# Half of the second MoE's output product in seven products, W_out of the first unit taken chunk by chunk, and a table that moves every group of a planned order

## The chip, the cores and the metric

The kernel runs on one core of one Trainium2 chip. The metric is the device time of one execution in microseconds (us); lower is better. The engines are TensorE (PE in the profile; its weight loads are PEld), VectorE (DVE), ScalarE (ACT), GpSimd (POOL) and SyncE (SP), which issues the DMAs.

## The reference

Three steps run one after the other; all inputs are fp32 or fp64 arrays.

```
q, k, v: (4, 8, 576, 64)            tau: scalar
scores = q @ k.T / 8;  keep scores >= max - tau;  attn = softmax of what is kept;  x = attn @ v
x  -> (2304, 512)
MoE 1:  r = relu(x @ w_in);   y = (s * r * r + b) @ w_out          # w_in (512, 2048), w_out (2048, 512)
MoE 2:  h = y @ w_in2;        out = (h * sigmoid(1.702 * h)) @ w_out2
```

## The kernel before

**Stages.** There are four batches of 576 tokens. Attention runs in eight units of 256 tokens (two for each batch, four head pairs each); the 64 last tokens of each batch are collected into a ninth unit. Unit 0 goes through MoE 1 in fp32 (`pair32`, then `bank32`), units 1 to 8 in pairs of fp16 parts, three matmuls for each product (`pair` L977, then `bank` L1065). MoE 2 runs over four blocks of 512 tokens and one of 256.

**MoE 2.** Its hidden product for a 512-token block is already done in seven products for each two by two group of quarters (`hidden7`, L1277, 256 columns a matmul, 8 calls of 42 matmuls a block); the 256-token block uses `hidden2` (L1333, 192 matmuls of 256 columns). The activation (`tanh`, L1229 on ScalarE and L1234 on VectorE) is cut into a high and a low fp16 part (L341 on ScalarE, L1240 on VectorE), which are the tiles `g`. The output product `rows2` (L1364) makes 128 tokens at a time: 48 matmuls of 512 columns, over four chunks of W_out with 12 each, 18 times in all. ScalarE scales the result (L341), and SyncE stores it.

**Weights.** Weights arrive as fp64 words of 8 bytes in `wst` tiles, are rebuilt as fp32 (`convert`, L778) and cut into fp16 parts. For W_out of MoE 1 this waits until unit 0, which uses the fp32 form, is done: `mlp` puts the four norms and one `scale_out` behind unit 0, and that cuts all four chunks in a row (`split_w`: 16 times L341 on ScalarE and L863 on VectorE).

**The order.** `Plan` holds every step with its engines, estimated cost and priority, and plays them forward: each engine takes the ready step of the lowest priority number whose buffers are free. What comes out is one fixed order for each engine, which the chip then follows with semaphores. So the estimates move no time by themselves; they move instructions. Priorities come from due times in the table `KN`. PSUM has four single banks `a`, one `d`, and three rotating ones (`y`, `yy`, from `bank_of`) in the last stage.

## Time and profile before

| | |
|---|---|
| median of 3 runs | 1019.95 us (1019.66 to 1020.05) |
| profiled execution, its own time | 1023.23 us |
| its span, first to last instruction | 1021.5 us |
| PE busy | 979.0 us (96%) |
| DVE busy | 694.9 us (68%) |
| ACT busy | 622.8 us (61%) |
| POOL busy | 207.3 us (20%) |
| granted TensorE clock, mean | 0.992 |

The span leaves 1.73 us of the profiled execution's own time outside. A matmul's recorded duration is a pipelined one: what a row of matmuls costs TensorE is read from the chain of work, where a run of them has its length and its count, not from the mean of one.

### The profile page before, as it was taken

To read this page: it belongs to the slowest core of one execution; us is meant where nothing else is said; L and a number is where in the kernel's file an instruction comes from. 1 tells how busy PE (TensorE), PEld (TensorE's weight loads), DVE (VectorE), ACT (ScalarE), POOL (GpSimd) and SP (SyncE) were. 2 spreads that over 40 slices of the span, in tenths; PEclk is the share of its full clock that TensorE was granted. 3 is DMA by queue.
4 is the path that set the end of the run, shared out by engine and by line. 5 is a ranking of instruction groups with operands and counts; after the bars stand their busy time and mean duration, and the time that the engine had idled before them with its cause. 6 is when DMAs were issued, how large, how long until landed. Compare 5 with 4: busy or idle time off the path is not lost.

```text
span 1021.5 us, 21133 instructions
## 1 busy us (share of the span) xinstructions
PE 979.0 (96%) x8181; PEld 723.0 (71%) x8181; DVE 694.9 (68%) x1538; ACT 622.8 (61%) x1194; POOL 207.3 (20%) x319
## 2 busy tenths in 40 slices
PE   5888999979999999999999999999999999999998
PEld 3556667757877777777778888886486486486483
DVE  5888688796778777886675888796366356356240
ACT  5777776587677666676555888694364355354250
POOL 2110034433443454444442000000001001000000
PEclk9999999999999999999999999999999999999999
DMA  7786267736668786776764257310010010000000
GB/s 258 260 287 220 68 167 176 172 66 160 123 136 210 157 165 126 151 169 144 148 105 83 93 175 237 131 49 1 32 53 1 31 53 1 31 32 1 31 12 21
DMA packets 173060, 115.84 MB, mean 113 GB/s; under 512 B 136536, under 2 KB 149920, under 8 KB 172960
## 3 DMA queue, kind: packets, MB, share of 16 engines
q1 hardware_dynamic: 172960, 114.50, 43.8%
q8 instruction: 64, 1.05, 0.4%
q14 instruction: 36, 0.29, 0.1%
HBM read 72.62 MB, written 10.00 MB: 81 GB/s over the span
## 4 chain that ended last, share of the span: by engine, by line
PE 74%; DVE 10%; ACT 7%; DMA 5%; issue 2%; POOL 0%; SPq 0%; ACTq 0%; DVEq 0%; POOLq 0%
PE a L1364 18%; PE yy L1065 11%; PE a L1277 8%; PE yy L977 7%; PE S L491 6%; PE y L977 4%; PE T L636 3%; PE y L1036 3%; PE yy L1277 3%; PE d L1277 2%; DVE e L541 2%; DMA wst<-in_moe_w_out 2%; DMA PT<-p 2%; DVE nm L515 2%; PE y L1277 2%
## 5 line engine op out<-in xcount | busy, mean ns | idle before, releaser
L977 PEld LDWEIGHTS <-wb 128*128 128x128 f16 x1536 | 147.8, 98 | 32.8 <-issue 15.9
L565 POOL TENSOR_TENSOR p<-e,p 128x512 f16<-128x512 f32 x108 | 128.5, 1190 | 204.3 <-ACT p L339 176.6
L1065 PEld LDWEIGHTS <-wb 128*128 128x128 f16 x1536 | 148.5, 98 | 26.7 <-issue 9.3
L1065 PE MATMUL yy<-g,wb 128*128 128x256 f16 x1248 | 146.3, 274 | 2.1 <-DVE g L354 1.7
L541 DVE SCALAR_TENSOR_TENSOR e<-S,tb,e 128x576 f32<-128x576 f32 x144 | 115.0, 814 | 47.4 <-ACT e L537 44.0
L1364 PE MATMUL a<-wb,g 128*128 128x512 f16 x648 | 145.2, 379 | 0.0
L1277 PEld LDWEIGHTS <-l 128*128 128x128 f16 x1344 | 131.5, 98 | 19.2
L515 DVE TENSOR_REDUCE nm<-S 128x1 f32<-128x576 f32 x144 | 104.5, 749 | 29.9 <-PE S L491 29.7
L1364 PEld LDWEIGHTS <-g 128*128 128x128 f16 x648 | 63.4, 98 | 72.1
L537 ACT ACTIVATE e<-S,tb 128x576 f32<-128x576 f32 x108 | 76.4, 735 | 56.7 <-DVE tb L529 47.1
L977 PE MATMUL yy<-xs,wb 128*128 128x256 f16 x888 | 104.2, 273 | 0.0
L1277 PE MATMUL a<-xs,l 128*128 128x256 f16 x768 | 96.4, 273 | 0.0
L339 ACT ACTIVATE p<-e 128x576 f16<-128x576 f32 x108 | 73.0, 677 | 32.9 <-DMA PT<-p 22.8
L977 PE MATMUL y<-xs,wb 128*128 128x256 f16 x648 | 78.6, 273 | 7.3 <-ACT gt L984 7.3
L341 ACT ACTIVATE gt<-a,x2y 128x512 f32<-128x512 f32 x18 | 12.4, 688 | 88.0 <-PE a L1364 64.8
L354 POOL TENSOR_TENSOR st<-wb 128x512 f32<-128x512 f32 x5 | 7.1, 1418 | 276.3 <-DVE gt L1234 123.0
L491 PE MATMUL S<-kk,qa 64*128 64x288 f32 (+1 forms) x320 | 54.6, 445 | 8.2 <-ACT kk L388 8.2
L1229 ACT ACTIVATE gt<-wb,x2h 128x256 f32<-128x256 f32 x64 | 36.4, 609 | 40.4 <-DVE wb L1296 37.8
L491 PE MATMUL S<-kk,qb 64*128 64x288 f32 (+1 forms) x320 | 57.6, 453 | 1.5 <-DVE e L541 1.4
L1289 ACT ACTIVATE wb<-a 128x256 f32<-128x256 f32 x96 | 36.3, 379 | 30.2 <-PE a L1277 29.7
L778 DVE SCALAR_TENSOR_TENSOR wb<-wst,tw 128x512 int32<-128x512 int32 x64 | 45.5, 713 | 6.6 <-ACT tw L339 6.0
L1364 PE MATMUL a<-wb 128*128 128x512 f16 x216 | 49.4, 379 | 0.0
(184 smaller groups left out, 1589.2 us busy)
## 6 DMA issues: line engine op xcount, KB each, us to landing
wst<-in_moe_w_in SPq DMA_DIRECT2D x32, 512.0 KB
wst<-in_moe_w_out SPq DMA_DIRECT2D x32, 512.0 KB
rv<-in_v SPq DMA_DIRECT2D x32, 320.0 KB
kk<-in_k SPq DMA_DIRECT2D x32, 288.0 KB
qb<-in_q SPq DMA_DIRECT2D x16, 288.0 KB
yd<-gt SPq DMA_DIRECT2D x18, 256.0 KB
wb<-yd SPq DMA_DIRECT2D x16, 256.0 KB
out<-gt SPq DMA_DIRECT2D x16, 256.0 KB
```

Of the source, the lines that this page charges most:

```text
L339: nc.scalar.activation(dst(), src(), AF.Copy)
L491: nc.tensor.matmul(Sp[to, half, :HALF], q[h][r, qcols], k[r, h * HALF : (h + 1) * HALF])
L515: {"DVE": 668.0}, lambda _: nc.vector.tensor_reduce(nm.ap, Sv(), AX.XY, ALU.min), [Sp], [nm],
L537: lambda _: nc.scalar.activation(ev(), Sv(), AF.Exp, bias=nm.ap if plain else nb(), scale=-1.0), [Sp, biased], [e],
L541: lambda _: nc.vector.scalar_tensor_tensor(ev(), Sv(), tb(), ev(), ALU.is_le, ALU.mult, accum_out=p["acc"][:, i, 0:1]),
L565: nc.gpsimd.tensor_tensor(p16[:, S + H2 :], e[:, :MAIN], p16[:, :MAIN], ALU.subtract)
L778: lambda _: nc.vector.scalar_tensor_tensor(stage[:, j, :].bitcast(I32), st.ap.bitcast(I32)[:, 1:1025:2], 13, flat(), ALU.logical_shift_rig ...
L977: nc.tensor.matmul(hps[:, h, :], W[:, i, j, kk * P : (kk + 1) * P], x[:, k, kk, :], start=t == 0, stop=t == len(terms) - 1,)
L1065: nc.tensor.matmul(yp[:, h, :], self.W[0, 1, c][:, i, j, i0 * P : (i0 + 1) * P], u["g"][c][:, k, j, :], start=t == 0, stop=t == len(terms) ...
L1229: lambda _, cols=cols, h=h: nc.scalar.activation(gt[:, cols], h(), AF.Tanh, scale=th[:, c : c + 1]),
L1277: nc.tensor.matmul(to(bank), W[:, u, m, j, kk * P : (kk + 1) * P], y[:, v, z, kk, :], start=n == 0 and not more, stop=n == 5, skip_group_c ...
L1364: nc.tensor.matmul(yp(), part(f, k), self.W[1, 1, f // CH][:, w, f % CH, :], start=n == 0, stop=n == 47,)
```

## The change

Five things differ. (1) Of MoE 2's W_out, chunks 2 and 3 (`pairs7`) are held as seven combinations (`seven_out`), the activations that meet them too (`seven_g`, four sums or differences and seven cuts for two rows of tiles), and `rows7` makes two tiles of 128 tokens together: 48 matmuls of 512 columns for chunks 0 and 1, and seven products of 12 matmuls of 256 columns for chunks 2 and 3. (2) The 256-token block goes through `hidden7` too, with 128 columns a matmul. (3) Unit 0 takes W_out of MoE 1 chunk by chunk for both output banks (`rows32`), the norms and scales stand ahead of it, and each chunk is cut behind its last use (`part_out`). (4) s and b are loaded behind the first k and q, and a one-column Exp on ScalarE stands at the start. (5) A table `MOVES` shifts the priority of each of some 760 groups of steps, several cost estimates are raised, and there are more buffers (`g` 8 for 6, `gt` 4 for 3, two of the `g` tiles lent from `wst`).

```diff
-    1, "g": 6, "wb": 9, "xs": 4, "gt": 3, "son": 1, "xon": 1, "gw": 1, "hs": 0.58, "hk": 2.1, "h4": 4, "scan": 2,
+    1, "g": 8, "gl": 2, "r7": 2, "no": -3.0, "rk": 0.5, "gon": 1, "wb": 9, "xs": 4, "gt": 4, "son": 1, "xon": 1, "gw": 1, "hs": 0.58, "hk": 2.1, "h4": 4, "scan": 2,
...
+MOVES = [
+    7, -135, -223, 203, 520, -20, 23, 47, 139, 20, -365, -464, -313, -1172, -1249, -1063, -1044, -412, -80, -123,
...
+        op["prio"] += 100.0 * MOVES[self.group] if self.group < len(MOVES) else 0.0
...
-        for i, src in enumerate((self.tau, self.s, self.b)):
-            nc.sync.dma_start(sc[:, i : i + 1], src.partition_broadcast(P))
-        self.s_ap, self.b_ap = sc[:, 1:2], sc[:, 2:3]
+        nc.sync.dma_start(sc[:, 0:1], self.tau.partition_broadcast(P))
+        warm = pool.tile([P, 1], F32, name="warm")
+        nc.scalar.activation(warm, self.ones[:, 0:1], AF.Exp)
...
+        if p["unit"] == p["hp"] == 0:
+            for i, src in ((1, self.s), (2, self.b)):
+                self.load(lambda i=i: self.scal_t[:, i : i + 1], lambda src=src: src.partition_broadcast(P), [self.scal], P * 4)
...
-        W = Buf(self.lp, "l16", [P, 2, 8, 2, 256], F16, NCH)
+        W = Buf(self.lp, "l16", [P, 2, 7, 2, 256], F16, NCH)
...
-        for c, stage in enumerate(stages):
-            self.W[m, 1, c] = self.split_w(stage, lambda c=c: sv["o"][:, c : c + 1], [sv["o"]])
+    def part_out(self, m, c, stage):
+        sv = self.scale_of(m)
+        scale = lambda: sv["o"][:, c : c + 1]
+        if m and c in self.pairs7:
+            self.W[m, 1, c] = self.seven_out(stage, scale, sv["o"])
+        else:
+            self.W[m, 1, c] = self.split_w(stage, scale, [sv["o"]])
+    def seven_out(self, stage, scale, scaled):
+
+        tiles = [Buf(stage.pool, stage.tag, [P, 2, 4, 2, 256], F16, stage.bufs) for _ in range(2)]
+        place = {name: (tiles[i // 4], i % 4) for i, name in enumerate(self.RIGHT)}
...
+        self.seven_b(
+            lambda name, src, reads: self.parted(*place[name], src, scale, reads + [scaled], place[name][1]),
+            b11, b12, b21, b22, t2, t3, q, of, 512,
+        )
+        return place
...
-    def bank32(self, u, ib):
+    def rows32(self, u, c):
...
+        if c == 0:
+            u["y"] = [self.bank_of([P, 2, n]) for _ in range(2)]
+        W, g = self.stage[0, 1, c], u["g"][c]
+        for ib, yp in enumerate(u["y"]):
+            for h in range(2):
...
+        if c in self.pairs7:
+            if r:
+                self.seven_g(blk, c, j, blk.pop("first"), gt)
+            else:
+                blk["first"] = gt
+            return
...
+    def seven_g(self, blk, c, j, g0, g1):
+
+        half = blk["n"] // 2
+        place = self.g7_of(blk, c, j)
+        of = lambda g, k: (lambda: g[:, k * half : (k + 1) * half])
+        a11, a21, a12, a22 = of(g0, 0), of(g0, 1), of(g1, 0), of(g1, 1)
+        p11, p21, p12, p22 = (g0, 0), (g0, 1), (g1, 0), (g1, 1)
+        cut = lambda name, src, part: self.parted(*place[name], src, 2.0 ** -18, [part], place[name][1], half)
+        any = dict(on=("DVE", None, "POOL")[KN["gon"]])
+        cut("a22", a22, p22)
+        self.sub(a22, a21, a22, [p21], [p22], half, op=ALU.add, **any)
+        cut("s1", a22, p22)
+        self.sub(a21, a11, a21, [p11], [p21], half, **any)
+        cut("a11", a11, p11)
+        self.sub(a11, a22, a11, [p22], [p11], half, **any)
+        cut("s3", a21, p21)
+        cut("a12", a12, p12)
+        self.sub(a12, a12, a11, [p11], [p12], half, **any)
+        cut("s2", a11, p11)
+        cut("s4", a12, p12)
+
...
-    def hidden2(self, blk, f):
...
+    def rows7(self, blk, t, pace):
...
+        Y, a, b = [self.single("a"), self.single("a")], self.single("d"), self.bank_of([P, 512])
+        flat = [c for c in range(NCH) if c not in self.pairs7]
...
+                    {"PE": (pe16(12, 512), 60.0)}, mm, [self.W[1, 1, c], tiles[c, 0][0], tiles[c, 1][0]] + [Y[r]] * (i > 0), [Y[r]],
...
+                    for u, v in ((0, 0), (0, 1), (1, 0)):
+                        nc.tensor.matmul(
+                            region(bank), g[:, u, z, rows], W[:, v, y, j, :], start=i == 0 and not more, stop=i == last,
+                            skip_group_check=True,
+                        )
+                        i += 1
...
+        product("a11", "b11", a, left, False, 0)
+        keep(0, 0)
+        product("s3", "t3", b, left, False, 1)
+        product("s2", "t2", a, left, True, 2)
+        keep(1, 0)
+        more(1, 0, 1)
+        product("a12", "b21", Y[0], left, True, 3)
+        product("s1", "t1", a, left, True, 4)
+        keep(0, 1)
+        more(1, 1, 0)
+        product("s4", "b22", Y[0], right, True, 5)
+        out(0)
+        product("a22", "t4", Y[1], left, True, 6)
+        out(1)
...
+            if u is plain[-1]:
+                for c in range(NCH):
+                    at(t + d + KN["no"], lambda c: self.norm(0, 1, c, self.stage[0, 1, c]), c)
+                at(t + d + KN["no"] + 0.01, self.scales_out, 0)
+            for c in range(NCH):
+                at(t + d + d * c / NCH, self.rows32, u, c)
+                if u is plain[-1]:
+                    at(t + d + d * c / NCH + 0.01, lambda c: self.part_out(0, c, self.stage[0, 1, c]), c)
...
-            at(t - 0.1, lambda c: self.norm(0, 1, c, self.stage[0, 1, c]), c)
-        at(t - 0.09, lambda: self.scale_out(0, [self.stage[0, 1, c] for c in range(NCH)]))
...
+            for f in range(0, F, 2):
+                at(t + e * KN["hs"] * f / F, self.hidden7, blk, f // 2, e * KN["hs"] * 2e3 / F)
+            rest, count = e * (1.0 - KN["hs"]), n // 2 // P
+            for i in range(count):
+                at(t + e * KN["hs"] + rest * i / count, self.rows7, blk, i, rest * 1e3 / count)
```

`seven_b` is the former body of `seven_x` (the seven right-hand combinations of x), now called for W_out as well; `small` hands out the first two narrow `g` tiles of a block from `wst`.

**SyncE at the start.** These are SyncE's first loads: the scalars tau, s and b (`scal`), the first head pair's k and q, the first weights. Before:

```order
L311 DMA scal<-in_tau 128x1
L311 DMA scal<-in_moe_s 128x1
L311 DMA scal<-in_moe_b 128x1
L358 DMA kk<-in_k 128x576
L358 DMA qa<-in_q 128x256
L358 DMA qb<-in_q 128x256
```

Now:

```order
L361 DMA scal<-in_tau 128x1
L415 DMA kk<-in_k 128x576
L415 DMA qa<-in_q 128x256
L415 DMA qb<-in_q 128x256
L415 DMA scal<-in_moe_s 128x1
```

The first k moved ahead of two small loads.

**ScalarE where W_out of MoE 1 is cut.** `wb<-wb,o_...` are the cuts of one chunk of W_out (four at a time), `gt<-y` reads a finished hidden bank of unit 1, `e` and `p` are attention. Before, the four chunks stand among unit 1's hidden banks:

```order
L388 ACTIVATE kk<-kk,qs 128x576
L341 ACTIVATE wb<-wb,o_2434 128x512 x4
L339 ACTIVATE p_2486<-e 128x576
L984 ACTIVATE gt<-y 128x512
L339 ACTIVATE rs<-T 64x256
L985 ACTIVATE gt<-gt 128x512
L341 ACTIVATE wb<-wb,o_2434 128x512 x4
L984 ACTIVATE gt<-y 128x512
```

Now, from the second chunk to the first hidden bank of unit 1 behind the cuts (L1097; the `gt<-y` of L393 empties an output bank of unit 0):

```order
L395 ACTIVATE wb<-wb,o_2129 128x512 x4
L393 ACTIVATE p_2347<-e 128x576
L393 ACTIVATE p_2379<-e 128x576
L609 ACTIVATE e<-S,tb 128x576
L395 ACTIVATE wb<-wb,o_2129 128x512 x4
L609 ACTIVATE e<-S,tb 128x576
L393 ACTIVATE p_2424<-e 128x576
L395 ACTIVATE wb<-wb,o_2129 128x512 x4
L393 ACTIVATE p_2455<-e 128x576
L448 ACTIVATE kk<-kk,qs 128x576
L393 ACTIVATE gt<-y 128x512
```

All four chunks' cuts moved ahead of unit 1's hidden banks, into unit 0's output product and the attention beside it.

**VectorE in the last block of MoE 2.** `gt<-gt,...` is the activation, `g<-gt,g` and `wb<-gt,wb` a low part. Before, in the middle of the 256-token block:

```order
L1234 SCALAR_TENSOR_TENSOR gt<-gt,y 128x256
L1240 SCALAR_TENSOR_TENSOR wb<-gt,wb 128x256
L1234 SCALAR_TENSOR_TENSOR gt<-gt,yy 128x256
L1240 SCALAR_TENSOR_TENSOR g<-gt,g 128x256
L1234 SCALAR_TENSOR_TENSOR gt<-gt,yy 128x256
```

Now, towards its end (L967 the seven low parts, L411 the sums and differences, L1345 the activation):

```order
L1345 SCALAR_TENSOR_TENSOR gt<-gt,wb 128x128
L1345 SCALAR_TENSOR_TENSOR gt<-gt,a 128x128
L967 SCALAR_TENSOR_TENSOR g<-gt,g 128x128 x2
L1345 SCALAR_TENSOR_TENSOR gt<-gt,wb 128x256
L967 SCALAR_TENSOR_TENSOR g<-gt,g 128x128 x3
L411 TENSOR_TENSOR gt<-gt 128x128 x3
L967 SCALAR_TENSOR_TENSOR g<-gt,g 128x128 x4
```

Where one low part stood for each activation, seven stand for two, with sums and differences between them.

## Rows read from the trace of the kernel before

**Rows 1.** Busy time by stage (start:end, length, engines, granted clock, DMA share, GB/s)

```profile
0.00:8.00 8.00, 0.00 (x0) 0.00 (x0) 0.62 (x6) 1.94 (x2) 2.71 (x11) 1.00 0.52 162
8.00:100.00 92.00, 78.81 (x495) 50.00 (x497) 78.09 (x174) 70.59 (x142) 11.12 (x35) 0.94 0.78 270
100.00:203.00 103.00, 99.66 (x768) 74.08 (x765) 80.88 (x198) 69.91 (x130) 31.05 (x53) 1.00 0.59 142
203.00:235.00 32.00, 23.76 (x251) 18.79 (x251) 28.42 (x58) 26.18 (x49) 11.70 (x14) 1.00 0.32 64
235.00:662.00 427.00, 422.02 (x4272) 344.90 (x4270) 325.69 (x716) 288.17 (x526) 142.33 (x202) 1.00 0.65 150
662.00:1017.00 355.00, 354.71 (x2405) 235.20 (x2405) 181.19 (x390) 165.50 (x349) 8.37 (x6) 1.00 0.07 25
```

**Rows 2.** Chain of work that ended last, MoE 2 (start us, us, what)

```profile
745.59 1.97 PE a L1277 x18
989.44 2.62 PE yy L1333 x24
995.99 20.73 PE a L1364 x96
1016.81 0.69 ACT gt L341
```

**Rows 3.** Timeline of TensorE, 203 to 235 us (last: idle before, releaser)

```profile
203.16 1.08 PE L812 MATMUL y<-wb 128*128 128x128 bf16 x16 [0.61 <-DVE n L822]
212.10 0.82 PE L977 MATMUL y<-xs,wb 128*128 128x256 f16 x6 [2.43 <-ACT gt L984]
216.87 0.81 PE L977 MATMUL y<-xs,wb 128*128 128x256 f16 x6 [1.78 <-ACT gt L984]
...
227.26 2.78 PE L977 MATMUL y<-xs,wb 128*128 128x256 f16 x24 [1.20 <-ACT gt L984]
```

**Rows 4.** Timelines of ScalarE and VectorE, same stretch

```profile
208.44 2.56 ACT L341 ACTIVATE wb<-wb,o 128x512 f16<-128x512 f32 x4 [2.06 <-DVE o L930]
...
210.12 3.63 DVE L863 SCALAR_TENSOR_TENSOR wb<-wb,o 128x512 f16<-128x512 f32 x4
```

**Rows 5.** Timeline of the start

```profile
1.20 0.42 SPq L311 DMA_DIRECT2D scal<-in_moe_s  x1
...
2.13 0.43 SPq L358 DMA_DIRECT2D kk<-in_k  x1
...
6.05 1.28 ACT L388 ACT_TABLE_LOAD   x1 [6.05 <-DMA kk<-in_k]
...
8.17 2.29 PE L491 MATMUL S<-kk,qa 64*128 64x288 f32 x8 [8.17 <-ACT kk L388]
```

**Rows 6.** Groups by form (count, busy us, mean ns, idle before)

```profile
L341 ACT ACTIVATE g<-gt 128x512 f16<-128x512 f32 x48 | 29.6, 626 | 5.8 <-DVE gt L1234 5.6
L341 ACT ACTIVATE g<-gt 128x256 f16<-128x256 f32 x12 | 5.0, 416 | 5.1 <-DVE gt L1234 5.1
L1090 ACT ACTIVATE gt<-yy,b,y 128x256 f32<-128x256 f32 x26 | 13.3, 556 | 7.9 <-PE yy L1065 7.9
L1240 DVE SCALAR_TENSOR_TENSOR g<-gt,g 128x512 f16<-128x512 f32 x48 | 35.5, 746 | 6.7 <-ACT g L341 6.7
L1240 DVE SCALAR_TENSOR_TENSOR g<-gt,g 128x256 f16<-128x256 f32 x12 | 5.1, 425 | 5.0 <-ACT g L341 4.8
L1296 DVE TENSOR_TENSOR wb<-wb,yy 128x256 f32<-128x256 f32 x40 | 16.2, 413 | 14.8 <-PE yy L1277 13.1 <-ACT wb L1289 1.7
```

**Rows 7.** The norm's matmuls, all of line 812 (ns min/median/max, first and last start us)

```profile
L812 PE MATMUL y<-wb x128: 217/218/233, 77.0 to 204.0; 128*128 128x128 bf16 x128
```

**Rows 8.** Weight loads, from the page's costliest groups

```profile
L1277 PEld LDWEIGHTS <-l 128*128 128x128 f16 x1344 | 131.5, 98 | 19.2
```

**Rows 9.** Busy time in the hidden products, a 512-token block and the last

```profile
740.30:773.80 33.50, 33.50 (x308) 29.93 (x306) 23.89 (x50) 21.93 (x51) 3.48 (x3) 1.00 0.11 40
975.00:996.00 21.00, 21.00 (x194) 18.77 (x192) 11.90 (x29) 12.91 (x31) 0.00 (x0) 1.00 0.04 14
```

More of the change, by code (lines that the diff above doesn't have):

```diff
@@ L341, in fn @@
                 nc.scalar.activation(dst(), src(), AF.Copy, scale=scale if isinstance(scale, float) else scale())
-        self.plan.add(self.some({"ACT": act(cols, psum) + (93 if callable(scale) else 0), "DVE": dve(cols, True, psum)}, also), fn, reads, writes, **kw)
+        engines = self.some({"ACT": act(cols, psum) + (93 if callable(scale) else 0) + more, "DVE": dve(cols, True, psum)}, also)
+        if wide:
+            engines["POOL"] = pool(cols, True)
+        self.plan.add(engines, fn, reads, writes, **kw)
     def some(self, engines, i):
@@ L1184, in seven_x @@
         tiles = [Buf(self.wp, "xs", [P, 2, 2, 2, half], F16, KN["xs"]) for _ in range(4)]
-        blk["x"] = [(tiles[i // 2], i % 2) for i in range(7)]
         quarter = lambda h, j: (lambda: xf[:, 2 * h : 2 * h + 2, half * j : half * j + half])
@@ L1342, in rows2 @@
-    def rows2(self, blk, i):
-        nc, add = self.nc, self.plan.add
-        yb = self.single("a")
-        yp = lambda: yb.ap
-        terms = [(f, i, k) for f in range(DFF // P) for k, i in ((0, 0), (1, 0), (0, 1))]
-        t, ys, sv = blk["t"], blk["ys"], self.scale_of(1)
-        tiles = {(c, j): self.g_of(blk, c, j) for c in range(NCH) for j in range(2)}
-        def part(f, k):
-            g, z = tiles[f // CH, f % 2]
-            return g[:, k, z, f % CH // 2, cols]
-        if i == 0:
+        half, now = n // 2, self.plan.prio
@@ L1354, in rows2 @@
+        ys, sv = blk["ys"], self.scale_of(1)
+        if t == 0:
             add(
                 self.tiny(1),
[L1356 to L1368 removed]
@@ new lines, in rows7, with mm @@
+        flat = [c for c in range(NCH) if c not in self.pairs7]
+        tiles = {(c, j): self.g_of(blk, c, j) for c in flat for j in range(2)}
+        steps = 2 * len(flat) + 7
+        at = lambda k: now + pace * k / steps
+        for r in range(2):
+            cols = slice(r * half + t * P, r * half + (t + 1) * P)
+            for i, c in enumerate(flat):
+                def mm(_, r=r, c=c, cols=cols):
+                    for f in range(CH):
+                        g, z = tiles[c, f % 2]
+                        for k, w in ((0, 0), (1, 0), (0, 1)):
+                            nc.tensor.matmul(
+                                Y[r].ap, g[:, k, z, f // 2, cols], self.W[1, 1, c][:, w, f, :],
+                                start=(c, f, k, w) == (flat[0], 0, 0, 0), stop=(c, f, k, w) == (flat[-1], CH - 1, 0, 1),
+                                skip_group_check=True,
+                            )
+                add(
+                    {"PE": (pe16(12, 512), 60.0)}, mm, [self.W[1, 1, c], tiles[c, 0][0], tiles[c, 1][0]] + [Y[r]] * (i > 0), [Y[r]],
+                    prio=at(r * len(flat) + i),
+                )
@@ new lines, in rows7, with product, mm @@
+        mine = [(c, j) for c in sorted(self.pairs7) for j in range(2)]
+        left, right = (lambda h: (lambda bank: bank[:, 256 * h : 256 * h + 256]))(0), (lambda bank: bank[:, 256:512])
+        rows = slice(t * P, (t + 1) * P)
+        def product(x, w, bank, region, more, k):
+            gs = [self.g7_of(blk, c, j)[x] for c, j in mine]
+            ws = [self.W[1, 1, c][w] for c, j in mine]
+            def mm(_):
+                i, last = 0, 3 * len(mine) - 1
+                for (c, j), (g, z), (W, y) in zip(mine, gs, ws):
+                    for u, v in ((0, 0), (0, 1), (1, 0)):
+                        nc.tensor.matmul(
+                            region(bank), g[:, u, z, rows], W[:, v, y, j, :], start=i == 0 and not more, stop=i == last,
+                            skip_group_check=True,
+                        )
+                        i += 1
+            reads = [(x, (u, z)) for x, z in gs + ws for u in range(2)]
+            add(
+                {"PE": (pe16(3 * len(mine), 256), 60.0)}, mm, reads + self.gate(b) * (bank is b) + [bank] * more, [bank],
+                prio=at(2 * len(flat) + k),
+            )
@@ new lines, in rows7, with keep, more @@
+        K = [Buf(self.wp, "gt", [P, 512], F32, KN["gt"]) for _ in range(2)]
+        soon = now - pace * KN["rk"]
+        def keep(r, h):
+            self.copy(
+                lambda: (right if h else left)(K[r]), lambda: left(a), [a, ys], [(K[r], h)], 256, scale=lambda: ys.ap, psum=True, prio=soon
+            )
+        def more(r, h, src):
+            add(
+                {"DVE": dve(256, psum=True)},
+                lambda _: nc.vector.scalar_tensor_tensor(
+                    (right if h else left)(K[r]), left(b), ys.ap, (right if h else left)(K[src]), ALU.mult, ALU.add
+                ),
+                [b, ys, (K[src], h)], [(K[r], h)], prio=soon,
+            )
@@ new lines, in out @@
+        def out(r):
+            add(
+                {"DVE": dve(512, psum=True)},
+                lambda _: nc.vector.scalar_tensor_tensor(K[r].ap, Y[r].ap, ys.ap, K[r].ap, ALU.mult, ALU.add),
+                [Y[r], ys, (K[r], 0), (K[r], 1)], [(K[r], 0), (K[r], 1)], prio=soon,
+            )
+            for part, dst in blk["rows"][r * half // P + t]:
+                self.load(lambda dst=dst: dst, lambda part=part: K[r][part], [], P * DM * 4, reads=[K[r]])
+        product("a11", "b11", a, left, False, 0)
```

255 lines of the change are left out of this document (127 added, 128 removed), and 34 rows, old and new, of tables (KN, MOVES).

## The prediction, made before the changed kernel was run

> **What bounds the kernel now.** I read the stages first [rows 1]. The reader is to see two halves. From 662 us to the end, TensorE is busy for 354.71 of 355 us at the full granted clock, while VectorE is busy for 181.19 and ScalarE for 165.50: MoE 2 is bound by TensorE and by nothing else. Before 662 us TensorE's idle time lies in three places: 8 us at the start, 13.2 us between 8 and 100 us, and 8.24 us (32.00 less 23.76) between 203 and 235 us; the 103 us between have 3.3, and the 427 us behind have 5.0. So the second half moves with what TensorE has to do, and the first with what the other engines hand it, and when.
>
> Then I read the chain of work for what a matmul costs there [rows 2]: 96 matmuls of 512 columns last 20.73 us, 215.9 ns each, and 24 of 256 columns last 2.62 us, 109.2 ns each (18 in 1.97 us, the same). With these two the stage can be rebuilt: 1344 and 192 matmuls of 256 columns and 18 x 48 = 864 of 512 make 146.8 + 21.0 + 186.5 = 354.3 us, the whole stage. So nothing is hidden in it, and a matmul less is time less.
>
> Third, the waits of 203 to 235 us [rows 3, 4]: TensorE waits 2.43, 1.78 and 1.20 us for ScalarE to empty a hidden bank, and ScalarE is then at four cuts of W_out in a row (2.56 us), each with a partner on VectorE (3.63 us for four). That is the place at which the four chunks are cut in one go.
>
> **The change, part by part.**
>
> *Seven products for chunks 2 and 3.* Nine times `rows7` replaces two calls of `rows2`: 96 matmuls of 512 columns become 48 of 512 and 7 x 12 = 84 of 256. In sum 186.5 us become 432 x 215.9 ns + 756 x 109.2 ns = 93.3 + 82.6 = 175.9 us: **-10.6 us**. Both widths have their own rows, so this term has little room.
>
> *The last block in seven products.* 192 matmuls of 256 columns (21.0 us) become 8 x 42 = 336 of 128. No matmul of MoE 2 has 128 columns. The nearest row is the norm of W_out, 16 matmuls of 128 columns in 1.08 us [rows 3], each of which is recorded with 218 ns [rows 7], so that they start (1.08 - 0.22)/15 = 57 ns apart. Bounds: half of 109.2, 54.6 ns (18.3 us), and 98 ns, the mean length of a weight load, if none could hide behind so short a matmul [rows 8] (32.9 us). I take 57 ns, since those 16 matmuls load other weights each too: 19.3 us, **-1.7 us**, between -2.7 and +11.9.
>
> *What the other engines do more in MoE 2.* For two activation tiles in chunks 2 and 3 there were two cuts of 512 columns; now there are seven of 256 and four sums. VectorE: 7 x 425 - 2 x 746 + 4 x 413 ns = 3.1 us; ScalarE: 7 x 416 - 2 x 626 ns = 1.7 us [rows 6]. Four times a block that is 12.5 and 6.6 us. I cost it at nothing: in the hidden stage of a block VectorE has 23.89 busy of 33.50 us [rows 9], so it ends some 3 us behind TensorE, and the 48 x 2 flat matmuls of the block (20.7 us) need none of it. If that cover were gone, 3 us a block would show, 12 us in all. In the last block the seven cuts are 128 wide, and VectorE and ScalarE have 11.90 and 12.91 busy of 21.00 us before [rows 9]. VectorE gets 28 low parts, 24 additions, 16 activations and 9 sums of 128 columns at an estimated 265 ns (425 less half of what 512 columns cost more than 256 [rows 6]) and 16 instructions of 256 at 425 ns, 27 us, against 19.3 us of hidden products, 10.4 us of flat ones and the last products of the block before. That is the tightest place.
>
> *A wait that is added.* In `rows7` three of the seven products use the one bank `d` in turn, and ScalarE must empty it between them. A row like it takes 556 ns [rows 6], and another product of 12 x 109.2 = 1310 ns stands between. Queued behind a late one is all of TensorE. 27 such handovers at 0 to 0.2 us each; I take **+1 us** for these and the last block together, between 0 and 12.
>
> *W_out of MoE 1.* The same 32 cuts are made, but now beside unit 0's fp32 output product, where TensorE has 99.66 of 103 us and VectorE and ScalarE 80.88 and 69.91 [rows 1]. There are 22 us of room on VectorE in that stage, and the cuts need about 4 x 3.63. Unit 1's hidden banks then meet no cuts. Of the 8.24 us I take **-6 us**: at best all of it, at worst nothing, if the cuts make attention late instead. `rows32` holds two of three banks while it runs; queued behind are unit 1's hidden products, which stood behind it before too.
>
> *The start.* k's first load goes from SyncE's fourth place to its second, 2.13 - 1.20 = 0.93 us earlier, and the 1.28 us of table load, which stood between k's landing and its scaling, are done while k is under way [rows 5]: **-2 us** of 2.2; at worst 0, if the loads of the weights are what sets the pace by 100 us (the DMA share there is 0.78 [rows 1]).
>
> *The table of 760 shifts, the costs and the buffers.* No row prices an order. What it can win at most of what shows is the idle time left before 662 us: 13.2 + 3.3 + 5.0 = 21.5 us [rows 1]; more may lie in stretches where isolated matmuls count as busy. What an order can lose is shown by 203 to 235 us: 8.24 us at one badly placed group. I choose a third of the first, **-7 us**, as nearer to the rows than either end, between -21.5 and +8.
>
> Sum: -10.6 - 1.7 + 1 - 6 - 2 - 7 = **-26.3 us**. The profiled execution took 1023.23 us, its span 1021.5; it becomes 996.9 us. The runs shown have a median of 1019.95, 3.3 us under it, so the prediction for them is **993.6 us**.
>
> The page "TensorE: Matmul & The Clock Gate" of the Trainium skill, section Back-to-back issue gap, speaks against the change: it gives a sustained spacing of about 131 ns for 512 columns and 81 for 128, which would make splitting a wide matmul into narrow ones a loss. By it the output product before would be an estimated 864 x 131 ns = 113 us, and the last block's 336 narrow matmuls 27.2 us. The trace disagrees for 512 columns (215.9 ns), and the page's own formula for a gap standing alone, N/2.4 + 2.5 ns, gives 215.8.
>
> **The rivals.**
>
> *Only TensorE's saving arrives.* The cuts that leave 203 to 235 us make attention late, and the new order wins and loses alike: -11.3 us, 1008.7 us. For it speaks that the engines' total work before 662 us is what it was; against it that the idle time of rows 3 has one visible cause and that this cause is moved.
>
> *The order wins most of the idle time.* All of 21.5 + 8.24 + 2.2 us, with the 11.3: 976.7 us. For it: VectorE and ScalarE are busy for only 78 and 71 of 92 us where TensorE idles most [rows 1], so none of them is full. Against: there the three wait for each other in turn, tile by tile.
>
> *Short matmuls are held by their weight loads.* Then the last block has 98 ns a matmul, +11.9 instead of -1.7: 1007.2 us. Against it are the 16 matmuls at 57 ns [rows 3]. The page named above would put this at 81 ns.
>
> *Slower: the handover of bank `d`.* If ScalarE stood behind its cuts whenever `d` is due, each of the 27 handovers could cost a cut or two. It decides at 27.3 us of other gains over 27 handovers: above 1.0 us each (two cuts of 416 ns and their waits) the kernel is slower; at 1.3 us it is at 1028 us. Against it: ScalarE is busy for 165.5 of 355 us [rows 1], and the rows stage is where it has least to do.
>
> **How the numbers follow.** The forecast (984 to 1003 us by its own bounds) has 0.52, TensorE's saving alone 0.20, most of the idle time won 0.20, weight loads 0.03, slower 0.05. The range from 974 to 1010 us holds the first four nearly whole, less the far ends of the second and third. A difference of 0.2% (2 us) is about what a measurement of this kernel can tell from no change. Faster: 0.94, within it 0.01, slower 0.05.
>
> **What would show it.** MoE 2, from its first hidden product to the last matmul, takes 355 us now and should take about 343; above 350 the handovers or the last block hold TensorE, and its row would show idle time before a product into `d` with ScalarE as the releaser, or before a 128-column matmul. That matmul should be spaced 55 to 60 ns. TensorE's first score should stand at about 6 us, not 8.17. The waits for ScalarE's `gt` in unit 1's hidden products should be gone, and MoE 2 should begin at about 647 us. I am wrong if it begins later than 658 us, since then the order gave back what the cuts and the start won; or earlier than 630.

## The result, and the profile after

The changed kernel took 1008.9 us (median of 6 runs, 1007.27 to 1013.42) beside 1018.92 us for the kernel before on the same chip: ratio 0.9916, 95% interval 0.9893 to 0.9940. It is faster by 10 us, where 26.3 were forecast. The profiled execution took 1013.42 us (span 1011.5), 4.5 us above its median, as that of before was 3.3 above the 1019.95 shown. So the two traces can be laid side by side, but no difference of a few us between single executions proves anything: 23 runs of the kernel before, in one later comparison, lay between 1013.33 and 1025.38 us. For sizes I use ratios.

The stages of the changed kernel, with the boundaries of [rows 1] (start:end, length, busy us of PE, PEld, DVE, ACT and POOL, granted clock, DMA share, GB/s):

```profile
0.00:8.00 8.00, 2.26 (x8) 1.18 (x8) 1.38 (x7) 2.28 (x4) 2.73 (x12) 1.00 0.63 186
8.00:100.00 92.00, 79.79 (x520) 47.58 (x518) 81.30 (x180) 70.99 (x144) 12.78 (x38) 0.98 0.78 273
100.00:203.00 103.00, 94.12 (x717) 70.67 (x714) 85.57 (x206) 70.68 (x129) 32.62 (x52) 0.98 0.58 131
203.00:235.00 32.00, 30.12 (x258) 23.41 (x258) 26.75 (x57) 29.67 (x57) 13.49 (x20) 1.00 0.82 187
235.00:662.00 427.00, 421.87 (x4274) 344.71 (x4273) 309.11 (x693) 283.41 (x522) 151.95 (x205) 1.00 0.61 142
662.00:1007.00 345.00, 343.31 (x2884) 267.42 (x2881) 259.28 (x613) 202.05 (x497) 38.33 (x38) 1.00 0.07 25
```

Read the PE column against [rows 1]. Between 203 and 235 us the idle time fell from 8.24 to 1.88 us, about as forecast. But between 100 and 203 us it rose from 3.3 to 8.9, between 8 and 100 us it is 12.2 where it was 13.2, and between 235 and 662 us 5.1 where it was 5.0. MoE 2, from 663.75 us (but for six matmuls at 657.7) to its last matmul, takes 342.7 us where it took 355. So the second half paid out, and the first did not.

Where the first half's gain went stands in the window 150 to 175 us. The kernel before:

```profile
150.00:175.00 25.00, 24.51 (x161) 19.95 (x162) 21.41 (x55) 16.55 (x31) 8.46 (x13) 1.00 0.71 162
```

The changed kernel:

```profile
150.00:175.00 25.00, 19.45 (x194) 14.39 (x192) 21.99 (x55) 16.17 (x31) 9.53 (x15) 0.93 0.55 133
```

VectorE and ScalarE are about as busy in both; TensorE has 0.5 us of idle time before and 5.55 after. What differs is the share of unit 0's output product in these 25 us. In the kernel before (L1036; the columns are PE, PEld, granted clock, DMA share, GB/s):

```profile
150.00:175.00 25.00, 17.87 (x78) 14.46 (x79) 1.00 0.71 162
```

In the changed kernel (L1151):

```profile
150.00:175.00 25.00, 0.51 (x2) 0.48 (x3) 0.93 0.55 133
```

TensorE's timeline there (last: idle before, releaser):

```profile
158.85 0.42 PE L677 MATMUL T<-ident,ri 128*64 128x128 f32 x2 [1.86 <-DVE rs L729]
...
163.89 0.32 PE L893 MATMUL y<-ident,n 128*128 128x128 f32 x1 [0.57 <-DVE n L888]
...
169.41 0.32 PE L893 MATMUL y<-ident,n 128*128 128x128 f32 x1 [1.36 <-DVE n L888]
170.26 1.08 PE L885 MATMUL y<-wb 128*128 128x128 bf16 x16 [0.52 <-DVE n L895]
...
173.59 0.41 PE L677 MATMUL T<-ident,ri 128*64 128x128 f32 x2 [0.85 <-DVE ri L649]
...
174.49 1.99 PE L1151 MATMUL y<-g,wb 128*128 128x256 f32 x8 [0.38 <-DVE n L895]
```

L885 and L893 are W_out's norms, L1151 is unit 0's output product. That product needs nobody's reply while it runs and is what filled TensorE in this stretch before, from 151.1 us on. Now it stands behind the four norms, in the same bank `y`, and begins at 174.5 us. Of the waits shown, 2.7 us end with attention's work on VectorE (`rs`, `ri`) and 2.8 us with the norms' own reductions (`n`).

The start and MoE 2 of the changed kernel, first from the timeline of the start:

```profile
0.73 1.28 ACT L363 ACT_TABLE_LOAD   x1 [0.73 <-PEq L1743]
...
1.21 0.41 SPq L415 DMA_DIRECT2D kk<-in_k  x1
...
5.74 2.29 PE L563 MATMUL S<-kk,qa 64*128 64x288 f32 x8 [5.74 <-ACT kk L448]
```

Then from the timeline of TensorE in the last block:

```profile
980.09 1.47 PE L1504 MATMUL a<-wb,g 128*128 128x256 f16 x12
981.40 0.50 PE L1416 MATMUL d<-xs,l 128*128 128x128 f16 x6
981.73 1.84 PE L1416 MATMUL a<-xs,l 128*128 128x128 f16 x30
```

The first score stands at 5.74 us instead of 8.17 [rows 5]. Thirty matmuls of 128 columns start (1.84 - 0.22)/29 = 56 ns apart. The group of the matmuls into `d`, and those of the cuts of the activation in MoE 2 (count, busy us, mean ns, idle before):

```profile
L1504 PE MATMUL d<-wb,g 128*128 128x256 f16 x306 | 38.8, 273 | 0.0
L967 DVE SCALAR_TENSOR_TENSOR g<-gt,g 128x256 f16<-128x256 f32 x105 | 50.3, 507 | 2.3 <-ACT g L395 2.1
L395 ACT ACTIVATE g<-gt 128x256 f16<-128x256 f32 x105 | 39.3, 410 | 28.0 <-DVE gt L411 18.1 <-POOL gt L411 8.1 <-DVE gt L1345 1.5
```

No handover of bank `d` cost TensorE anything: no idle time before 306 matmuls into it. The only wait of TensorE in MoE 2 that shows is at its beginning, the seam of the two halves, from the timeline of all engines:

```profile
673.28 3.09 DVE L967 SCALAR_TENSOR_TENSOR wb<-wb,o 128x512 f16<-128x512 f32 x3
...
675.74 0.66 ACT L1428 ACTIVATE wb<-a 128x256 f32<-128x256 f32 x2 [1.14 <-DVE wb L967]
676.17 0.81 PE L1416 MATMUL a<-xs,l 128*128 128x256 f16 x6 [1.08 <-ACT wb L1428]
```

These are cuts of MoE 2's own W_out (`seven_out`, L967 and L395): two chunks now need seven cuts and four sums each instead of four cuts. The prediction has no term for them.

### The profile page after: what moved, and what is told of

The parts are those of the page before. It is cut to its first block, busy times and chain, and to the rows that moved or that the text cites. A ratio compares the mean times of both kernels' runs of the same rounds, so it can differ in the third digit from the quotient of the medians.

```text
span 1011.5 us, 22501 instructions
## 1 busy us (share of the span) xinstructions
PE 971.5 (96%) x8649; PEld 755.0 (75%) x8649; DVE 763.6 (75%) x1752; ACT 659.1 (65%) x1349; POOL 251.9 (25%) x362
## 4 chain that ended last, share of the span: by engine, by line
PE 74%; DVE 12%; DMA 6%; ACT 5%; issue 2%; SPq 1%; POOL 0%; DVEq 0%; ACTq 0%
PE a L1483 9%; PE a L1416 9%; PE yy L1183 9%; PE yy L1090 7%; PE S L563 7%; PE y L1090 5%; PE T L708 5%; PE a L1504 3%; PE d L1504 3%; PE y L1183 3%; PE yy L1416 3%; PE y L1151 2%; PE d L1416 2%; DMA wst<-in_moe_w_in 2%; DVE l L967 2%
## 5 line engine op out<-in xcount | busy, mean ns | idle before, releaser
L1416 PEld LDWEIGHTS <-l 128*128 128x128 f16 x1680 | 150.7, 98 | 18.8 <-issue 1.5
L1416 PE MATMUL a<-xs,l 128*128 128x256 f16 (+1 forms) x960 | 109.5, 262 | 1.1 <-ACT wb L1428 1.1
L1090 PE MATMUL yy<-xs,wb 128*128 128x256 f16 x888 | 107.1, 275 | 1.0 <-ACT gt L1208 1.0
L393 ACT ACTIVATE p<-e 128x576 f16<-128x576 f32 x108 | 73.0, 679 | 38.4 <-DMA PT<-p 21.6
L411 POOL TENSOR_TENSOR gt<-gt 128x256 f32<-128x256 f32 (+1 forms) x23 | 18.8, 822 | 267.9 <-DVE gt L411 200.7
L1504 PEld LDWEIGHTS <-g 128*128 128x128 f16 x714 | 69.5, 98 | 10.1
L395 ACT ACTIVATE g<-gt 128x256 f16<-128x256 f32 (+2 forms) x137 | 49.4, 394 | 30.7 <-DVE gt L411 19.8
L1428 ACT ACTIVATE wb<-a 128x256 f32<-128x256 f32 (+1 forms) x120 | 41.4, 357 | 30.2 <-PE a L1416 28.1
L967 DVE SCALAR_TENSOR_TENSOR g<-gt,g 128x256 f16<-128x256 f32 (+1 forms) x133 | 58.0, 466 | 2.7 <-ACT g L395 2.5
L1340 ACT ACTIVATE gt<-wb,x2h 128x256 f32<-128x256 f32 (+2 forms) x80 | 44.4, 577 | 10.4 <-DVE wb L1435 9.7
L1483 PE MATMUL a<-wb,wst 128*128 128x512 f16 x216 | 48.9, 380 | 0.0
```

Source lines behind the costliest of these rows:

```text
L393: nc.scalar.activation(dst(), src(), AF.Copy)
L967: lambda _: nc.vector.scalar_tensor_tensor(lo(), src(), by(), hi(), ALU.mult, ALU.subtract),
L1090: nc.tensor.matmul(hps[:, h, :], W[:, i, j, kk * P : (kk + 1) * P], x[:, k, kk, :], start=t == 0, stop=t == len(terms) - 1,)
L1416: nc.tensor.matmul(to(bank), W[:, u, m, j, kk * P : (kk + 1) * P], y[:, v, z, kk, :], start=n == 0 and not more, stop=n == 5, skip_group_c ...
L1483: nc.tensor.matmul(Y[r].ap, g[:, k, z, f // 2, cols], self.W[1, 1, c][:, w, f, :], start=(c, f, k, w) == (flat[0], 0, 0, 0), stop=(c, f, k ...
L1504: nc.tensor.matmul(region(bank), g[:, u, z, rows], W[:, v, y, j, :], start=i == 0 and not more, stop=i == last, skip_group_check=True,)
```

## The experiments

Two kinds. Where the planner may choose anew, one edit changes the whole order behind it. Where "its order is kept", the planner sees the same steps and only what a step issues differs.

**1. One part of the change alone, or one part less, planned anew.**

MoE 2's part alone:

```
-MOVES = [ 7, -135, ... ]          +MOVES = []
 # start, cost estimates, W_out of MoE 1 (bank32, four norms and cuts behind unit 0) as before
```

> Only the MoE 2 part of the change (seven products in the output product of chunks 2 and 3 and in the last block, with the buffers they need); start, planner's costs, table of shifts and W_out of MoE 1 as in the kernel before. Theory 'idle only moved' (all that the change does before 662 us sums to nothing): the same as the whole change, 1007 to 1011 us, ratio to the kernel before 0.989 to 0.993, MoE 2 in 342 to 345 us. Rival 'the first half has parts of both signs' (start and W_out won their 8 us and the table lost as much): also about 1009, so this run alone fixes only the size of the MoE 2 term; above 1012 it would say that the first half did win something, below 1006 that it lost.

Measured: 1017.24 us, ratio 0.9988 (0.9965 to 1.0011). That is above 1012, but not because the change's first half wins something: hardly anything of MoE 2's 12 us is left, and its window at the seam shows why (columns as above):

```profile
655.00:690.00 35.00, 28.70 (x235) 24.13 (x233) 33.83 (x68) 27.81 (x56) 3.56 (x3) 0.90 0.02 9
```

The longest wait in it, from TensorE's timeline:

```profile
677.28 1.44 PE L1373 MATMUL a<-xs,l 128*128 128x256 f16 x6 [3.52 <-ACT wb L1385]
```

The kernel before, in the same window:

```profile
655.00:690.00 35.00, 35.00 (x324) 31.43 (x323) 33.25 (x73) 31.40 (x67) 0.00 (x0) 1.00 0.13 46
```

TensorE idles 6.3 of 35 us, with a granted clock of 0.90 in the mean, so part of the rest is at the lower level, 1.2 GHz (six matmuls last 1.44 us here, 0.82 us elsewhere); before the change it had 35.00 of 35 busy. VectorE was nearly full before too (33.25, now 33.83), so its load alone is not the cause. The order in its queue can be, with the cuts of W_out ahead of the results of the first hidden products; the third group of runs tests that.

The whole change without the table:

```
-MOVES = [ 7, -135, ... ]          +MOVES = []
```

> The whole change with the table of shifts emptied, nothing else. 'Idle only moved': the sum of TensorE's lost time by 240 us is set by VectorE's and ScalarE's work for attention, so the order changes little: 1006 to 1012 us. Rival 'the table lost what the cuts and the start won': without it 8 us come back, 998 to 1002 us. Rival 'the table carries the gain, and the other edits of the first half cost time without it': 1014 us or more.

Measured: 1047.34 us, ratio 1.0280 (1.0245 to 1.0314). This is the third theory. The table is worth 37 us in this kernel, and the other edits together, MoE 2's part among them, cost 28.5 without it.

W_out of MoE 1 back in one go:

```
-    at(t + d + KN["no"], norm, c)             +    at(t + 2 * d - 0.1, norm, c)        # no shift
-    at(t + d + d * c / NCH + 0.01, part_out)  +    at(t + 2 * d - 0.09, part_out)
```

> The whole change, but norms, scales and cuts of W_out of MoE 1 at the place of before, in one go behind unit 0's output product; every other job keeps its shift. 'Idle only moved': the hole of 150 to 175 us (5.5 us of idle TensorE) closes, one of about 8 us opens between 203 and 235 us, and the time stays within 2.5 us of 1009. Rival 'the chunk by chunk cuts won 6 us that the table lost elsewhere': 1013 to 1017 us. Rival 'the cuts in front of unit 0's output product are what lost': 1003 us or less.

Measured: 1016.7 us, ratio 0.9983 (0.9963 to 1.0003), 6.8 us more than the change, clear of its interval; the second theory's number. Its trace, first unit 0's output product alone between 150 and 175 us (L1151, columns as above), then all engines:

```profile
150.00:175.00 25.00, 16.23 (x71) 13.10 (x72) 1.00 0.60 156
```

```profile
150.00:175.00 25.00, 25.00 (x174) 19.83 (x172) 20.77 (x49) 17.32 (x33) 9.93 (x15) 1.00 0.60 156
203.00:235.00 32.00, 23.35 (x215) 17.10 (x216) 26.70 (x64) 23.62 (x42) 7.07 (x11) 0.89 0.35 61
235.00:662.00 427.00, 418.12 (x4245) 342.23 (x4244) 313.76 (x691) 285.09 (x526) 158.60 (x214) 1.00 0.64 148
```

The output product is back, and the hole of 150 to 175 us is closed, with attention's work still beside it: so it is the missing filler that opens it. The hole between 203 and 235 us is open again (8.65 us). Between 100 and 245 us this order idles 4.1 us more than the change's (14.9 against 10.8), and behind 245 us another 2.3 us (7.4 against 5.1), at places to which the edit does not reach. So under the table the new place of W_out does win, about 4 of the 6 us that were forecast; the rest of the 6.8 us may be the table's fit to it.

The start of before, planned anew:

```
+    for i, src in enumerate((tau, s, b)): dma_start(sc[:, i], src)      # ahead of k
-    warm = activation(ones, Exp);  load s, b behind the first q
```

> The whole change with the start of before (s and b loaded ahead of k, no early table load for the exponential). 'The start was given back by 20 us' (the first tiles are paced by loads and by VectorE, not by the first score): the first score is back at about 8.2 us and the time within 1 us of 1009. Rival 'the start's 2 us arrived and something else lost them': 1010.5 to 1012 us.

Measured: 1035.11 us, ratio 1.0160 (1.0127 to 1.0193), far outside both. Two loads in another place and one instruction less are no 25 us of work. In its trace TensorE has these windows, where the change has 34.45 of 40 and 27.91 of 30 us busy:

```profile
150.00:190.00 40.00, 28.81 (x208) 21.25 (x206) 33.98 (x86) 21.80 (x39) 14.57 (x21) 0.83 0.66 162
...
570.00:600.00 30.00, 21.68 (x196) 17.56 (x195) 15.39 (x28) 13.76 (x27) 4.45 (x6) 0.77 0.28 73
```

The order fell apart 150 and 570 us behind the edit: the shifts were fitted to one list of steps, and a small change of it cost 25 us. So this run prices the table's fit and not its edit.

**2. The change's order kept.**

The old start again, now with every engine's order as it is (the planned loads of s and b issue nothing):

```
+    for i, src in enumerate((tau, s, b)): dma_start(sc[:, i], src)
-    warm = activation(ones, Exp)
+    plan.steps[-1]["fn"] = lambda _: None       # the planned loads of s and b
```

> The changed kernel with every engine's order kept as it is, and only the start of before: s and b are loaded ahead of k, and the exponential's table is not loaded early. (The run before this one with the old start let the planner choose anew, and so changed the whole order.) Theory 'given back by 30 us': first score at about 8.2 us, and the time within 1 us of the changed kernel's 1008.9, ratio 0.990 to 0.9935. Rival 'the start's 2 us arrive': 1010.5 to 1011.5 us, ratio near 0.994. Rival 'TensorE's later start shifts everything': 1011.4 us.

Measured: 1011.1 us, ratio 0.9921 (0.9891 to 0.9951) against 0.9916: no loss shows, though the first score is back at 8.38 us. The interval also holds the rival's 0.994, so "given back" is likely and not settled. Then the work that stands in the hole:

```
-    for o in range(CH): ... matmul(N[:, o], w, w)      +    (none for W_out of MoE 1)
-    reduce, transpose, reduce                          +    memset(n2, 0.25)
```

> The changed kernel with its order kept, leaving out the norm of W_out of MoE 1: its 64 bf16 products and 4 transposes on TensorE and 8 reductions on VectorE are gone, a constant stands in for the norm. Theory 'the chain of norms on the one bank y holds the output product behind it': the 5.5 us of idle TensorE in 150 to 175 us go, and with the norms' own 5.5 us of TensorE and 4 us of VectorE the time falls by 8 to 11 us, to 998 to 1001. Rival 'attention on VectorE and ScalarE sets the pace there, whatever TensorE has to do': the idle time stays or grows, and the time falls by less than 4 us, 1005 or more.

Measured: 1007.58 us, ratio 0.9884 (0.9852 to 0.9917), some 3 us less, with intervals that overlap, and TensorE's idle time in the window of the hole grew from 5.55 to 6.63 us:

```profile
150.00:175.00 25.00, 18.37 (x135) 13.93 (x135) 21.51 (x58) 16.80 (x30) 10.33 (x16) 0.93 0.70 164
```

So the waits that ended with the norms' reductions were not what made the hole: without them TensorE waits for attention's replies instead. Together with the run that put the filler back, it is a missing filler in front of these replies. Is it one engine's work that makes them late? VectorE first, then ScalarE:

```
-    tensor_reduce(mx, rv, max)                 +    memset(mx, 4.0)
```

> The changed kernel with its order kept, leaving out VectorE's search for the largest value of v (16 reductions of 0.81 us, 12 of them before 240 us); a constant of 0.06 us stands in. 9 us of VectorE's work before 240 us are gone, nothing of TensorE's. Theory 'VectorE's work sets the pace to 240 us': 5 to 9 us less than the changed kernel, ratio to before 0.983 to 0.987. Rival 'the pace is set by the replies between the engines, or by the loads, and VectorE has room': less than 3 us, ratio 0.9887 or more.

```
-    activation(k, k, Copy, scale=qs)           +    activation(k[:, 0:1], k[:, 0:1], Copy, scale=qs)
```

> The changed kernel with its order kept, leaving out ScalarE's scaling of k but for one column (32 times 0.78 us, 16 of them before 240 us): some 10 us of ScalarE's work before 240 us are gone. 'VectorE sets the pace': within 2.5 us of the changed kernel, ratio 0.989 to 0.993. Rival 'ScalarE sets it, or both alike': 4 to 9 us less, ratio 0.983 to 0.988.

Measured: 0.9890 (0.9872 to 0.9908) and 0.9891 (0.9873 to 0.9910), about 2.6 us less each for 9 and 10 us of work left out, with intervals that overlap the change's. Neither engine sets the pace by itself; for VectorE that leaves the rival with the replies or the loads, and ScalarE's run is at the edge of its first range, whose theory the run on VectorE speaks against.

**3. The seam at 660 to 690 us.**

The cuts for chunks 2 and 3 later, in the change and in MoE 2's part alone:

```
-    at(t + KN["so2"], part_out, 1, c)          +    at(t + KN["so2"] + (20.0 if c > 1 else 0.0), part_out, 1, c)
```

> The changed kernel with one due time moved: the cuts of W_out of MoE 2 for the chunks 2 and 3 (seven cuts and four sums each, used first at about 714 us) are due 20 us later; the order differs only from about 660 us on. Theory 'the seven cuts stand in front of the first hidden products' results': the 1.1 us of idle TensorE at 676 us goes and the time falls by 1 to 2.6 us. Rival 'they are hidden, and later they hold the first output product': the same or up to 5 us slower.

> The kernel with the MoE 2 part alone, with the same later cuts for chunks 2 and 3. There TensorE is idle for 5.1 us at 672 to 677 us and has the lower clock around it. Theory 'the cuts of W_out into seven, which the sum left out, took back two thirds of MoE 2's gain': 6 to 9 us less than without the move, 1008 to 1011 us. Rival 'the cuts are not what holds TensorE there': 1015 us or more.

Measured: 0.9946 (0.9923 to 0.9968), 3 us slower than the change, and 0.9976 (0.9950 to 1.0002), 1.2 us less than without the move; in both pairs the intervals overlap. The first trace has 3.7 us of idle TensorE between 655 and 690 us where the change has 1.1. Later in one row is no cure: in the second, TensorE's longest wait (2.7 us, for ScalarE's `wb`) moved to 687 us. Then MoE 2's part with the new start, the cuts spread, and the sums on VectorE:

```
-    at(t + KN["so2"], part_out, 1, c)          +    at(t + KN["so2"] + 12.0 * c, part_out, 1, c)
-    "xon": 1                                   +    "xon": 0          # sums of seven_out on VectorE alone
```

MoE 2's part and the new start, nothing else:

> The kernel with the MoE 2 part alone, and with the new start (k's first load second, the exponential's table loaded early, s and b behind); no table, costs and W_out as before. MoE 2 alone had ratio 0.9988. 'Given back by 30 us': within 2 us, 0.997 to 1.001. Rival 'the start's 2 us arrive without the table': 0.9965 or less.

The same, cuts spread:

> MoE 2 part and new start alone (ratio 0.9948), with the cuts of MoE 2's W_out spread: chunk by chunk, each due 12 us after the last. 'Cuts in a row hold the hidden products' results': the 9 us that this kernel loses at 660 to 690 us shrink to 2 to 4, 1006 to 1009 us, ratio 0.987 to 0.991. Rival 'VectorE and ScalarE have too much to do in the first block, in whatever order': 1011 us or more, ratio above 0.992.

The same, cuts spread and sums on VectorE:

> As the run with spread cuts, and the eight sums of W_out of MoE 2 are made by VectorE alone (0.68 us each) instead of by GpSimd too (1.6 us each, beside which a cut on VectorE took 1.76 us for 0.74). 'GpSimd beside VectorE is what costs': 2 to 4 us less than with spread cuts alone. Rival 'it takes work from VectorE, which is full there': the same, or up to 3 us slower.

Measured: 1013.14, 1008.55 and 1001.85 us, ratios 0.9948 (0.9930 to 0.9966), 0.9886 (0.9855 to 0.9918) and 0.9832 (0.9803 to 0.9861). The seam of the first of the three:

```profile
655.00:690.00 35.00, 29.28 (x244) 24.93 (x245) 33.83 (x73) 29.66 (x62) 1.62 (x1) 0.90 0.02 9
```

and of the last:

```profile
655.00:690.00 35.00, 34.93 (x309) 30.00 (x308) 32.71 (x72) 29.88 (x66) 1.39 (x1) 1.00 0.03 9
```

With VectorE about as busy, TensorE loses 0.07 us instead of 5.72. **The last of these kernels beats both: 17.5 us less than before, 1.7%, with no table at all.** The run with the cuts spread alone has a full seam too (35.00 of 35 us), but it loses 2.3 us just behind it, where the last one loses 0.2; first that run, then the last:

```profile
700.00:730.00 30.00, 27.69 (x202) 19.51 (x201) 26.08 (x50) 12.87 (x30) 9.43 (x9) 1.00 0.16 54
```

```profile
700.00:730.00 30.00, 29.82 (x227) 22.01 (x225) 26.50 (x59) 14.76 (x31) 3.39 (x4) 1.00 0.15 54
```

So spreading closes the seam, and the sums on VectorE close what it leaves, 2.1 us by the traces; the times give 5.5 us, but the intervals of these two runs touch. In the change, whose seam the table had already eased (1.1 us; the whole change without the table loses 5.3 us at its own seam, between 700 and 710 us), the sums on VectorE alone do nothing that shows:

> The changed kernel with one thing changed: the eight sums of W_out of MoE 2 on VectorE alone; the order differs from about 660 us on. 'GpSimd beside VectorE costs': the 1.1 us of idle TensorE at 676 us go, 1 to 3 us less than the change, ratio 0.988 to 0.9905. Rival 'VectorE is full there': the same or up to 3 us slower, 0.991 to 0.995.

Measured: 0.9905 (0.9872 to 0.9939).

**4. The remaining parts without a table.**

The new cost estimates with MoE 2's part:

```
-    {"ACT": act(S) + 93.0}, {"DVE": dve(376)}, {"POOL": 300.0}, {"DVE": 130.0}, {"ACT": 624.0}, ...
+    {"ACT": act(S) + 160.0}, {"DVE": dve(490)}, {"POOL": 360.0}, {"DVE": Shared(200.0)}, {"ACT": 650.0}, ...
```

> The MoE 2 part alone (ratio 0.9988) with the planner's new cost estimates, no table, start and W_out as before. 'The new costs send the planner on a worse order, which the table repairs': new idle time of TensorE between 440 and 640 us, 1030 us or more. Rival 'costs and order are harmless by themselves, and only together with W_out's new place they lose': within 4 us of 1017.

Measured: 1037.55 us, ratio 1.0175 (1.0144 to 1.0205): 19 us of loss by numbers that change no instruction. One wait in its timeline shows the kind of loss, the last pair of attention with no filler left:

```profile
574.72 3.20 PE L670 MATMUL T<-PT,V 128*64 128x256 f16 x27 [5.91 <-DMA PT<-p]
```

W_out of MoE 1 chunk by chunk, added to MoE 2's part and then to the best kernel (the edit of `mlp` shown ahead of the prediction, without table and costs):

```
+    at(t + d + KN["no"], norm, c);  scales_out
+    at(t + d + d * c / NCH, rows32, u, c);  part_out behind each
```

> The kernel with the MoE 2 part alone, and with W_out of MoE 1 chunk by chunk as in the change (norms 3 us ahead of unit 0's output product, each cut behind that chunk's products); no table, costs and start of before. MoE 2 alone had ratio 0.9988. Theory 'the work is moved, the hole with it': within 3 us of that, 0.996 to 1.002, with less idle time at 203 to 235 us and more at 150 to 175. Rival 'it wins its 6 us where no table is in the way': 0.993 or less. Rival 'the planner's new order is worse': above 1.005.

> The best kernel so far (ratio 0.9832) with W_out of MoE 1 chunk by chunk as in the change added, no table, costs as before. 'The norms and cuts ahead of unit 0's output product lose more than the hole behind it gives': 1004 us or more, ratio above 0.986, with TensorE idle at 150 to 190 us. Rival 'it wins its 6 us': 998 us or less, ratio below 0.9795. 'The hole only moves': between the two.

Measured: 1.0013 (0.9994 to 1.0032) against 0.9988, and 0.9902 (0.9875 to 0.9929) against 0.9832: 2.5 us more in the first pair, which is within the intervals, and some 7 us more in the second, which is not. MoE 2's part with W_out in one go:

```profile
150.00:190.00 40.00, 40.00 (x266) 31.89 (x266) 30.82 (x72) 25.71 (x46) 15.98 (x25) 1.00 0.81 190
203.00:235.00 32.00, 24.64 (x330) 19.95 (x331) 28.59 (x58) 27.24 (x52) 11.82 (x13) 1.00 0.27 60
```

and chunk by chunk:

```profile
150.00:190.00 40.00, 31.07 (x232) 23.61 (x233) 37.97 (x97) 23.68 (x42) 15.03 (x21) 0.87 0.69 157
203.00:235.00 32.00, 30.16 (x260) 22.90 (x259) 27.33 (x53) 27.00 (x51) 11.72 (x15) 1.00 0.63 159
```

The second window wins 5.5 us of TensorE and the first loses 8.9. VectorE shows why it can't be free: the work that came into the first window makes it 37.97 busy of 40 us. In the second pair the same windows differ less (2.5 us lost, 1.9 won), so they show the direction and not the 7 us. Last, the best kernel with the old start:

```
 # as the best kernel, with s and b ahead of k and no early table load
```

> The best kernel so far (MoE 2 part, new start, cuts of MoE 2's W_out spread, their sums on VectorE; ratio 0.9832) with the old start. 'The start's 2 us arrive where no table was fitted to another order': 1004 to 1006 us, ratio 0.985 to 0.988. Rival 'given back by 30 us': within 1 us of 1001.9, ratio 0.982 to 0.9845.

Measured: 0.9878 (0.9853 to 0.9903) against 0.9832: the start is worth some 4.7 us there, if the planner may build on it (the intervals touch; MoE 2's part with and without the new start gave 4.1 us). This kernel is also MoE 2's part with a clean seam and nothing else: 12.5 us less than before.

## Why the prediction was right in one half and wrong in the other

The time came out where the rival "Only TensorE's saving arrives" had put it (1008.7 us), inside the range, and my forecast was 15 us too low. The rival's mechanism holds in the main: MoE 2's saving arrived and the first half netted nothing. That it netted so nearly nothing is luck, since it is the sum of large terms of both signs. MoE 2 began at 663.75 us; 647 was forecast, and later than 658 was to mean that the first half had given its gains back.

**Seven products: right.** -10.6 and -1.7 us were forecast for MoE 2, and the stage went from 355 to 342.7 us with 1.1 of idle time in it. The 128-column matmuls have 56 ns where 57 was taken; the handovers of `d` cost 0 instead of +1; VectorE's extra cuts of the activation stayed hidden (259.28 busy of 345 us). The run with MoE 2's part and a clean seam gives 12.5 us as a time, with an interval of 2.5 us to either side.

**W_out of MoE 1, "-6 us": the step that failed.** I counted the hole that the cuts leave, and "22 us of room on VectorE" where they go, as a sum over a stage of 103 us. But that stage was full only because unit 0's output product filled TensorE while attention's replies came. Moved behind the norms, it left a hole: 203 to 235 us gave 6.4 us of idle time back, and 100 to 203 us took 5.5, so 0.8 us came out where 6 was forecast. I also wrote that `rows32` holds two of three banks; both its products and the norms use the one bank `y` in turn (the rows at 169 to 175 us), so the norms put the filler off, to 174.5 us. What the edit is worth as a time depends on the order around it: under the table, taking it out cost 6.8 us, some 4 of them where its cuts stand; without the table, putting it in cost 2.5 to 7 us. So it failed as an addend: the hole that it closes and the hole that it opens are of about the same size, and the order around them decides which is larger.

**"The table, the costs and the buffers, -7": wrong in kind.** I took a third of the idle time that shows, 7 of 21.5 us, as if the order before were a base on which a table can only win or lose a little. Of that idle time, what lies at 8 to 100 and at 235 to 662 us fell by 0.8 us. The runs show two large opposite sizes: the costs +19, all edits of the first half without table +28.5 (with MoE 2's 12 in it), the table -37. The sum of such terms is not to be read from the idle time of the old kernel. So with W_out this is the second term that failed, and which of the 760 shifts do the repair is open.

**The start, "-2": right in place, unsettled in size.** The first score stands at 5.74 us. In the change's order that is worth nothing that can be measured (0.9921 against 0.9916); without a table it goes with 4.1 and 4.7 us, more than the 2.4 us of the first score, so part of that is the new order that the planner makes of it.

**A missing term.** MoE 2's W_out now needs 22 cuts and 8 sums instead of 16 cuts, at the moment at which its first hidden products want the same two engines. In the change this costs 1.1 us of idle time; in MoE 2's part alone it took back nearly all of the gain, 11 of the 12.5 us that came with a clean seam.

Open: what holds attention's replies at 100 to 240 us. Leaving out work of VectorE or ScalarE, or the norms on TensorE and VectorE, gave about a third of that work or less, so it is probably a chain through several engines. GpSimd's part and the DMA transposes were not tried, and no run here shows which link to shorten.

## What to carry to other kernels

Before counting a hole as a gain, ask what fills the stage into which its cause is moved: work that waits for nobody is worth more there than the busy time says. Where a planner sets the order, an edit's price is that of the whole new order; try each part alone with the order kept, and each with a new order, before a table is fitted to all of them. And when weights get more cuts, look at the seam at which they are made: here spreading them, in a kernel without a table, ended below the kernel with it.
